# Strided Q/K loads, a re-ordered first FFN group, filler matmuls and an earlier range check in a one-core attention + FFN kernel

## The chip, the cores and the metric

The kernel runs on one core of a Trainium2 chip. The metric is the device time of one execution in microseconds (us). The core has five engines that run side by side, each through its own queue of instructions in the order of the program: TensorE (PE, matmuls and transposes, with weight loads shown as PEld), VectorE (DVE), ScalarE (ACT), GpSimd (POOL) and SyncE (SP, which here only issues DMAs). Every engine waits on semaphores for what others produce.

## The reference

Sliding-window causal attention (window 64) over 8 batches, 8 heads, 576 positions and head size 64, and behind it a multiplicative FFN with two linear layers after the product:

```python
scores = (q @ k.T) / 8                       # per batch and head
mask = (rel >= 0) & (rel < 64)               # rel = query position - key position
attn = softmax(where(mask, scores, -1e9))
x = (attn @ v) as [4608, 512]                # heads side by side
a = x @ w1                                   # 512 -> 1024
b = x @ w2                                   # 512 -> 1024
out = ((a * b) @ w3) @ w_out                 # 1024 -> 1024 -> 512, float32
```

## The kernel before

**Attention.** One batch is cut into 3 query segments of 192 positions and 4 pairs of heads, so 12 units u for each batch and 96 in all (`NU`). `scores(u)` makes two matmuls into PSUM `s_ps` (2 buffers), ACT takes the exponential of it with a fixed shift into the half-precision tile `pt` (4 buffers), and two `affine_select` groups on POOL (L271, L273) put zeros outside the window. `values(u)` makes four matmuls of V with `pt` into `o_ps` (2 buffers). V carries columns of ones, so that the sums of the exponentials come out beside the values; ACT takes their logarithm (L298, L299, into `ln_s`) and the exponential of its negative (L301, `r`), and DVE multiplies (L304, L305) into `xT`, the transposed attention output in a ring of four batches. `values` runs two units behind `scores` (`LAG = 2`). `tick(u)` is one step of both, plus the events that prepare the next batch (`late`, `second`).

**Q and K.** `load_qk` fills a float32 tile `stage` (4 buffers, shared with the weights) in four DMAs, one for each pair of heads, each to 32 partitions; a partition holds 18 positions. `cast_qk` casts half of it to half precision, `transposes` turns 6 of the 18 positions at a time: six PE transposes into one PSUM tile (`tp`, one buffer; for batch 0 `f_ps`, three buffers), then copies into `kT` (one on DVE) or `qT` (one on ACT and one on DVE, L247).

**V.** `load_v` issues five DMAs a batch from POOL, which cast on the way; `copy_v` makes block 1 from blocks 0 and 2, and half of block 4, on DVE.

**FFN.** w3 and w_out are multiplied together once (the fold, 8 steps: `fold_t` transposes 128 rows of w3, `fold_mm` multiplies with w_out), so that a group of 512 rows takes 8 steps `ffn_ab` (8 matmuls of 128x512 each, an ACT copy L379, a DVE product L380) and 4 steps `ffn_o` (8 matmuls, a DVE copy L388, a store from SP). There are 9 groups. w1, w2, w_out and w3 come as float32 megabytes through `stage` and are cast on POOL or DVE. Before the fold, w3's half-precision rows lie in the space of the first product tile and in a part of `xT` that batch 2 needs later.

**Order.** The schedule is written by hand: what is emitted first comes first in each engine's queue. Batch 0's attention runs alone in a loop (L462). Then a list of FFN steps (`slots`, 20 for group 0 with its fold, 12 for each other group) is gone through; each has a due unit, and behind each step ticks run until `u` has reached its due. In group 0 the steps before `first` have no tick behind them. The functions hung on a step by `at` run ahead of it: batch 1's casts at step 3, its k transposes at step 4, its q transposes at step 5.

**The range check.** The fixed shift of the exponential is only right if the logarithms lie in a range. `keep_sums` sends two rows of `ln_s` by DMA from SP into `lnsum` for each segment of each batch; at the end (L557 to L567) DVE squares and compares them, a small matmul adds up the flags and `bad_i` holds the count. All engines load it (L570), and a branch leads to a slow general path that these inputs do not take.

Of the kernel before, what the change touches and what calls it, by code (L numbers as in the profile page):

```python
# [15 lines left out]
P = 128  # L16
# [128 lines left out]
def kernel(  # L145
# [54 lines left out]
    def load_qk(b, which):  # L200
        src = k if which == "k" else q
        t = sb.tile([P, 2, TI * D], FP32, name="stage", bufs=4)
        for j in range(NJ):
            nc.sync.dma_start(out=t[j * TP:(j + 1) * TP],
                              in_=src[b, 2 * j:2 * j + 2].rearrange("h (p r) d -> p h (r d)", r=TI))
# [25 lines left out]
    def transposes(b, which, c, early=False):  # L231
# [7 lines left out]
        src = tp.rearrange("q i (j p) -> q j p i", p=TP)  # L239
# [37 lines left out]
    def values(u):  # L277
# [17 lines left out]
        if j == 0:  # L295
            lns[b, si] = sb.tile([P, NJ, 192], FP32, name="ln_s", bufs=3)
# [46 lines left out]
    def tick(u):  # L343
# [10 lines left out]
        if (u - LAG - 4) % 4 == 3 and u - LAG - 4 >= 8:  # L354
# [72 lines left out]
    def fold_t(fc):  # L427

        w3 = w3_rows(fc).rearrange("p a (e n) -> p (a e) n", n=P)
        tp = ps_t.tile([P, 8, P], FP16, name="tp")  # L430
# [11 lines left out]


# [7 lines left out]
    for v16 in v16s:  # L451
        nc.gpsimd.memset(v16.rearrange("p c j (a e) -> p (c j a) e", a=2)[:, :, D:2 * D], 1.0)
    wst = [load_w12(moe_w1, 0), load_w12(moe_w2, 0)]
    for which in "kq":
# [4 lines left out]
    for c in VLOADS.values():  # L459
        load_v(0, c)  # L460
    wst += [load_w12(moe_w1, 1), load_w12(moe_w2, 1)]
    for u in range(12 + LAG):  # L462
# [4 lines left out]
        if u == 5:  # L467
            pool_cp(w2_sb[:, :, 0:512], wst[1])
        if u == 6:
            dve_cp(w1_sb[:, :, 0:512], wst[0])  # L470
            load_qk(1, "k")
            load_qk(1, "q")
        if u == 10:
            pool_cp(w2_sb[:, :, 512:1024], wst[3])
            dve_cp(w1_sb[:, :, 512:1024], wst[2])
# [4 lines left out]
        if u in (9, 13):  # L480
            keep_sums((u - 9) // 4)
# [5 lines left out]
    for g in range(NG):  # L487
        part = [lambda g=g, fc=fc: ffn_ab(g, fc) for fc in range(8)]
        first = 0
        if g == 0:  # L490
            first = 5
# [15 lines left out]
            def casts_b1():  # L507
                for which in "kq":
                    for hh in range(2):
                        cast_qk(1, which, hh, pool_cp if hh else act_cp)  # L510

            def load_b1():
                for c in VLOADS.values():
                    load_v(1, c)
                for half in range(2):
                    stg["o", half] = load_wo(half)
                for n in range(4):
                    stg["3", n] = load_w3(n)
                    if n == 1:
                        for half in range(2):  # L520
                            pool_cp(wo16[:, 4 * half:4 * half + 4, :], stg["o", half])
                    if n >= 2:
                        cast_w3(n - 2, stg["3", n - 2], pool_cp)

            def more_w3(n):
                cast_w3(n, stg["3", n], pool_cp)

            part += [lambda fc=fc: fold_step(fc) for fc in range(8)]
            at(3, casts_b1)
            at(4, load_b1)  # L530
            at(4, lambda: [transposes(1, "k", c) for c in range(3)])
# [72 lines left out]
```

## Time and profile before

| | |
|---|---|
| median of three runs | 345.68 us (345.57 to 347.91) |
| the profiled execution | 346.64 us, of which the span from the first to the last instruction is 344.8 us |
| PE busy | 280.1 us, 1922 matmuls |
| DVE, ACT, POOL busy | 214.4, 211.9, 211.9 us |
| moved by DMA | 44.15 MB |

The profile is one execution. A row of the timeline gives the start, the duration, the engine, the line of the kernel, the operation with its output and input tile and shape, the count of instructions merged into the row, and in brackets how long the engine was idle before and what ended that. Merged rows can overlap the next row. A row of the stages gives the stretch, its length, the busy time of PE, PEld, DVE, ACT and POOL, the granted TensorE clock, the mean busy share of the DMA engines, and GB/s. In the list of costly groups, the numbers behind the count are busy us, mean ns of one, and idle time before. In the list of waits the columns are the total of us, the times and the longest. The strip of PE has 40 slices of 8.6 us, in tenths busy.

### The profile page before, as it was taken

What the parts mean: (1) busy time and instruction counts of PE and PEld (TensorE: products, weight loads), DVE (VectorE), ACT (ScalarE), POOL (GpSimd) and SP (SyncE); (2) the same over time, 40 slices, a digit from 0 to 9 for tenths busy, and PEclk for the clock granted to TensorE, in tenths of its full rate; (3) what the DMA queues carried; (4) which work ended last, traced back from release to release, by engine and by line L of the source; (5) the groups of instructions that cost most, each with busy time, mean ns of one, the idle gap of its engine ahead of it and who ended that gap; (6) DMA issues with size and microseconds to landing.
All of it is one profiled execution on the core that took longest, in us unless ns stands there. A gap on an engine that the chain in (4) does not pass through costs nothing.

```text
span 344.8 us, 5950 instructions
## 1 busy us (share of the span) xinstructions
PE 280.1 (81%) x1922; PEld 161.2 (47%) x1922; DVE 214.4 (62%) x393; ACT 211.9 (61%) x493; POOL 211.9 (61%) x343
## 2 busy tenths in 40 slices
PE   0425557476886799999999999999999999999950
PEld 0312323234544355555555558956555555554420
DVE  4334644526344676679789778757887876564432
ACT  1237844244553557878989887659978987843200
POOL 6375996426695465768997995659789564420000
PEclk9999999878999899999999999999999999999995
DMA  8999999997395059949977985259309202012030
GB/s 180 286 325 38 202 303 167 414 220 80 26 209 79 30 141 232 53 111 224 117 128 170 161 108 159 45 69 238 25 33 147 18 23 102 0 47 80 0 122 11
DMA packets 52201, 44.15 MB, mean 128 GB/s; under 512 B 39312, under 2 KB 39312, under 8 KB 52160
## 3 DMA queue, kind: packets, MB, share of 16 engines
q1 hardware_dynamic: 14656, 38.95, 41.6%
q0 software_dynamic: 37504, 4.72, 26.5%
q8 instruction: 17, 0.28, 0.4%
q14 instruction: 24, 0.20, 0.2%
HBM read 38.80 MB, written 9.44 MB: 140 GB/s over the span
## 4 chain that ended last, share of the span: by engine, by line
PE 68%; DVE 8%; POOL 8%; DMA 6%; ACT 4%; issue 3%; SPq 1%; DVEq 0%; ACTq 0%; POOLq 0%
PE f_ps L376 33%; PE f_ps L386 18%; PE o_ps L289 5%; PE tp L238 4%; PE s_ps L260 4%; DMA v<-in_v_dram 3%; PE f_ps L440 3%; DMA stage<-in_q_dram 3%; POOL pt L271 2%; POOL pt L273 2%; DVE kT L242 1%; DVE ab L380 1%; DVE qT L247 1%; ACT pt L264 1%; DVE xT L305 1%
## 5 line engine op out<-in xcount | busy, mean ns | idle before, releaser
L376 PE MATMUL f_ps<-xT,w_sb 128*128 128x512 f16 (+1 forms) x640 | 137.7, 366 | 1.7 <-DVE xT L305 0.6
L271 POOL TENSOR_SCALAR_AFFINE_SELECT pt<-pt 128x512 f16<-128x512 f16 (+2 forms) x128 | 65.3, 510 | 70.4 <-ACT pt L264 70.0
L376 PEld LDWEIGHTS <-w_sb 128*128 128x128 f16 x640 | 61.3, 99 | 56.1 <-issue 7.5
L264 ACT ACTIVATE pt<-s_ps 128x512 f16<-128x512 f32 (+1 forms) x96 | 53.7, 561 | 30.2 <-PE s_ps L260 25.7
L273 POOL TENSOR_SCALAR_AFFINE_SELECT pt<-pt 128x512 f16<-128x512 f16 (+2 forms) x128 | 64.4, 503 | 8.8
L386 PE MATMUL f_ps<-wc_sb,ab 128*128 128x512 f16 x288 | 68.6, 385 | 0.0
L304 DVE TENSOR_TENSOR xT<-o_ps,r 64x192 f16<-64x192 f32 x96 | 33.4, 348 | 55.5 <-ACT r L301 53.6
L380 DVE TENSOR_TENSOR ab<-f_ps,a_sb 128x512 f16<-128x512 f32 x72 | 49.7, 692 | 24.1 <-PE f_ps L376 21.4
L379 ACT COPY a_sb<-f_ps 128x512 f32<-128x512 f32 x72 | 41.3, 574 | 27.2 <-PE f_ps L376 27.2
L289 PE MATMUL o_ps<-pt,v 128*128 128x128 f16 (+1 forms) x384 | 38.0, 224 | 16.6 <-POOL pt L273 6.8
L298 ACT ACTIVATE ln_s<-o_ps 64x192 f32<-64x192 f32 x96 | 31.5, 328 | 17.5 <-PE o_ps L289 15.4
L386 PEld LDWEIGHTS <-ab 128*128 128x128 f16 x288 | 27.0, 99 | 28.2 <-issue 1.4
L260 PE MATMUL s_ps<-qT,kT 128*128 128x256 f16 x192 | 37.4, 281 | 3.1 <-DVE qT L247 2.4
L289 PEld LDWEIGHTS <-v 128*128 128x128 f16 x384 | 27.5, 101 | 22.6 <-issue 6.9
L301 ACT ACTIVATE r<-ln_s 128x192 f32<-128x192 f32 x96 | 34.9, 363 | 3.0
L305 DVE TENSOR_TENSOR xT<-o_ps,r 64x192 f16<-64x192 f32 x96 | 34.6, 361 | 1.3
L220 POOL DMA_DIRECT2D v<-in_v_dram x40 | 34.3, 862 | 1.7 <-DVE xT L305 1.1
L299 ACT ACTIVATE ln_s<-o_ps 64x192 f32<-64x192 f32 x96 | 31.0, 323 | 1.1
L260 PEld LDWEIGHTS <-kT 128*128 128x128 f16 x192 | 19.5, 104 | 22.7 <-issue 4.9
L388 DVE COPY t2k<-f_ps 128x512 f32<-128x512 f32 x36 | 24.9, 692 | 7.4 <-PE f_ps L386 6.5
L247 DVE COPY qT<-tp 64x768 f16<-64x768 f16 x21 | 20.2, 961 | 9.9 <-ACT qT L247 9.6
L242 DVE COPY kT<-tp 128x768 f16<-128x768 f16 x21 | 20.0, 951 | 4.2 <-PE tp L238 4.2
(52 smaller groups left out, 196.5 us busy)
## 6 DMA issues: line engine op xcount, KB each, us to landing
stage<-in_k_dram SPq DMA_DIRECT2D x32, 288.0 KB, 4.4
stage<-in_q_dram SPq DMA_DIRECT2D x32, 288.0 KB, 7.9
out_dram<-t2k SPq DMA_DIRECT2D x36, 256.0 KB, 2.0
stage<-in_moe_w_dram SPq DMA_DIRECT2D x8, 1024.0 KB, 10.6
v<-in_v_dram POOLq DMA_DIRECT2D x32, 128.0 KB, 4.4
stage<-in_moe_w_out_dram SPq DMA_DIRECT2D x2, 1024.0 KB
v<-in_v_dram POOLq DMA_DIRECT2D x8, 64.0 KB, 4.6
lnsum<-ln_s SPq DMA_DIRECT2D x24, 6.0 KB
```

The lines of the kernel that those rows point to most:

```text
L220: nc.gpsimd.dma_start(out=vh[lo:P, c], in_=v[b, :, s0:s0 + P - lo, :].rearrange("h s d -> s h d"))
L260: nc.tensor.matmul(s_ps[:, c0:c0 + 2 * n].rearrange("k (a n) -> k a n", a=2), kT[:, j, k0:k0 + P], qT[:, j, :, q0:q0 + n], start=True, sto ...
L264: nc.scalar.activation(pt[:, 0:2 * w], s_ps[:, 0:2 * w], AF.Exp, bias=-SHIFT, scale=scale)
L271: nc.gpsimd.affine_select(out=sl, in_=sl, pattern=[[step, nb], [0, 2], [1, n]], compare_op=ALU.is_ge, fill=0.0, base=off, channel_multipli ...
L273: nc.gpsimd.affine_select(out=sl, in_=sl, pattern=[[-step, nb], [0, 2], [-1, n]], compare_op=ALU.is_ge, fill=0.0, base=63 - off, channel_m ...
L289: nc.tensor.matmul(o_ps[:, a, q0 - q_base:q0 - q_base + n], v16[:, si * 2 + bi, j, a * D:a * D + P], pt[:, c0 + a * n:c0 + a * n + n], sta ...
L301: nc.scalar.activation(r, y[:, j], AF.Exp, scale=-1.0)
L305: nc.vector.tensor_tensor(xs[D:P], o_ps[D:P, 1, :], r[D:P], ALU.mult)
L376: nc.tensor.matmul(d[:, lo:hi], w[:, dc, fc * P:(fc + 1) * P], xT[:, dc, xc:xc + hi - lo], start=(dc == 0 and ci == 0), stop=(dc == 3), sk ...
L379: act_cp(a_sb, a_ps)
L380: nc.vector.tensor_tensor(ab[:, fc, :], b_ps, a_sb, ALU.mult)
L386: nc.tensor.matmul(o_ps, ab[:, fc, t * P:t * P + P], wc_sb[:, fc, :], start=(fc == 0), stop=(fc == 7))
```

## The change

- `load_qk` writes each pair of heads to every fourth partition (j, j+4, ...) instead of 32 adjacent ones, and the copies behind the transposes read PSUM in that order.
- Batch 0's start: the first V block is loaded between the two fills of ones; `keep_busy(n)` issues n matmuls of the identity with itself into `tp` that nobody reads: 45 ahead of the first cast, 20 behind the transposes of k and of q, 8 in each step of batch 0's loop.
- The casts of w2's first half move from POOL to DVE; the second halves of w1 and w2 are cast on DVE behind the first step of group 0. The loads of batch 1's Q and K stand one step later in the loop, and its first V block is loaded there.
- Group 0: batch 1's casts, V loads and transposes and the casts of w_out and w3 are handed out to single steps (`todo`, run behind the step), one group of transposes to a step from step 2 to step 7. w3's second half is loaded behind the casts of the first. No tick runs in the first eight steps (`first = 8`, it was 5).
- The fold's transposes use `f_ps` (three buffers) instead of `tp` (one).
- `ln_s` has four buffers; batch 0's three `keep_sums` come in group 0's steps 1 to 3.
- The last group's steps are due five units later, which finishes the ticks behind its first step; the range check is emitted behind its fifth step instead of at the end.

```diff
@@ -201,7 +201,7 @@
         src = k if which == "k" else q
         t = sb.tile([P, 2, TI * D], FP32, name="stage", bufs=4)
         for j in range(NJ):
-            nc.sync.dma_start(out=t[j * TP:(j + 1) * TP],
+            nc.sync.dma_start(out=t[j:P:NJ],
                               in_=src[b, 2 * j:2 * j + 2].rearrange("h (p r) d -> p h (r d)", r=TI))
         raws[which, b] = t
 
@@ -236,7 +236,7 @@
         tp = ps_f.tile([P, 6, P], FP16, name="f_ps") if early else ps_t.tile([P, 6, P], FP16, name="tp")
         for i in range(6):
             nc.tensor.transpose(tp[:, i, :], t16[:, 6 * c + i, :], ident16)
-        src = tp.rearrange("q i (j p) -> q j p i", p=TP)
+        src = tp.rearrange("q i (p j) -> q j p i", p=TP)
         if which == "k":
             cp = act_cp if early and c == 1 else dve_cp
             cp(kTs[b].rearrange("q j (p i) -> q j p i", i=TI)[:, :, :, 6 * c:6 * c + 6], src)
@@ -293,7 +293,7 @@
                 first = False
                 c0 += 2 * n
         if j == 0:
-            lns[b, si] = sb.tile([P, NJ, 192], FP32, name="ln_s", bufs=3)
+            lns[b, si] = sb.tile([P, NJ, 192], FP32, name="ln_s", bufs=4)
         y = lns[b, si]
         nc.scalar.activation(y[0:D, j], o_ps[D:P, 0, :], AF.Ln)
         nc.scalar.activation(y[D:P, j], o_ps[0:D, 1, :], AF.Ln)
@@ -351,7 +351,7 @@
                 event(b, *e)
         if 12 <= u - LAG < NU:
             values(u - LAG)
-        if (u - LAG - 4) % 4 == 3 and u - LAG - 4 >= 8:
+        if (u - LAG - 4) % 4 == 3 and u - LAG - 4 >= 12:
             keep_sums((u - LAG - 4) // 4)
         for e in ev:
             if e[0] != "t":
@@ -427,7 +427,7 @@
     def fold_t(fc):
 
         w3 = w3_rows(fc).rearrange("p a (e n) -> p (a e) n", n=P)
-        tp = ps_t.tile([P, 8, P], FP16, name="tp")
+        tp = ps_f.tile([P, 8, P], FP16, name="f_ps")
         for ec in range(8):
             nc.tensor.transpose(tp[:, ec, :], w3[:, ec, :], ident16)
         w3T = sb.tile([P, 8, P], FP16, name="t2k", bufs=4)
@@ -440,6 +440,27 @@
             nc.tensor.matmul(o_ps, w3T[:, ec, :], wo16[:, ec, :], start=(ec == 0), stop=(ec == 7))
         act_cp(wc_sb[:, fc, :], o_ps)
 
+    def check_sums():
+
+        rows = 2 * 3 * B
+        chk = const.tile([rows, NJ * 192], FP32)
+        nc.vector.tensor_tensor(chk, lnsum, lnsum, ALU.mult)
+        nc.vector.tensor_single_scalar(chk, chk, BOUND * BOUND, op=ALU.is_le)
+        okv = const.tile([rows, 1], FP32)
+        nc.vector.tensor_reduce(okv, chk, axis=mybir.AxisListType.X, op=ALU.min)
+        nc.vector.tensor_scalar(okv, okv, -1.0, 1.0, op0=ALU.mult, op1=ALU.add)
+        ones = const.tile([rows, 1], FP32)
+        nc.vector.memset(ones, 1.0)
+        c_ps = ps_t.tile([1, 1], FP32, name="tp")
+        nc.tensor.matmul(c_ps, okv, ones, start=True, stop=True)
+        nc.vector.tensor_copy(bad_i[0:1, :], c_ps)
+
+
+    def keep_busy(n):
+
+        d = ps_t.tile([P, P], FP32, name="tp")
+        for _ in range(n):
+            nc.tensor.matmul(d, ident16, ident16, start=True, stop=True)
 
     load_qk(0, "k")
     load_qk(0, "q")
@@ -448,15 +469,20 @@
     for qT in qTs:
         nc.vector.memset(qT[D:P, :, 0, :], 0.0)
         nc.vector.memset(qT[0:D, :, 1, :], 0.0)
-    for v16 in v16s:
+    vl = list(VLOADS.values())
+    for i, v16 in enumerate(v16s):
         nc.gpsimd.memset(v16.rearrange("p c j (a e) -> p (c j a) e", a=2)[:, :, D:2 * D], 1.0)
+        if i == 0:
+            load_v(0, vl[0])
     wst = [load_w12(moe_w1, 0), load_w12(moe_w2, 0)]
+    keep_busy(45)
     for which in "kq":
         cast_qk(0, which, 0, dve_cp)
         cast_qk(0, which, 1, act_cp if which == "k" else pool_cp)
         for c in range(3):
             transposes(0, which, c, early=True)
-    for c in VLOADS.values():
+        keep_busy(20)
+    for c in vl[1:]:
         load_v(0, c)
     wst += [load_w12(moe_w1, 1), load_w12(moe_w2, 1)]
     for u in range(12 + LAG):
@@ -465,20 +491,18 @@
         if u == 7:
             copy_v(0, 4)
         if u == 5:
-            pool_cp(w2_sb[:, :, 0:512], wst[1])
-        if u == 6:
             dve_cp(w1_sb[:, :, 0:512], wst[0])
+        if u == 7:
+            dve_cp(w2_sb[:, :, 0:512], wst[1])
             load_qk(1, "k")
             load_qk(1, "q")
-        if u == 10:
-            pool_cp(w2_sb[:, :, 512:1024], wst[3])
-            dve_cp(w1_sb[:, :, 512:1024], wst[2])
+        if u == 8:
+            load_v(1, vl[0])
         if u < 12:
             scores(u)
         if u >= LAG:
             values(u - LAG)
-        if u in (9, 13):
-            keep_sums((u - 9) // 4)
+        keep_busy(8)
     u = 12
 
 
@@ -488,7 +512,7 @@
         part = [lambda g=g, fc=fc: ffn_ab(g, fc) for fc in range(8)]
         first = 0
         if g == 0:
-            first = 5
+            first = 8
             w3Ts, stg = {}, {}
 
             def fold_step(fc):
@@ -504,67 +528,61 @@
                     f()
                 part[n] = both
 
-            def casts_b1():
-                for which in "kq":
-                    for hh in range(2):
-                        cast_qk(1, which, hh, pool_cp if hh else act_cp)
-
-            def load_b1():
-                for c in VLOADS.values():
-                    load_v(1, c)
+            def late_w12(i):
+                dve_cp((w1_sb, w2_sb)[i][:, :, 512:1024], wst[2 + i])
+
+            def first_w3():
                 for half in range(2):
                     stg["o", half] = load_wo(half)
-                for n in range(4):
+                for n in range(2):
                     stg["3", n] = load_w3(n)
-                    if n == 1:
-                        for half in range(2):
-                            pool_cp(wo16[:, 4 * half:4 * half + 4, :], stg["o", half])
-                    if n >= 2:
-                        cast_w3(n - 2, stg["3", n - 2], pool_cp)
 
             def more_w3(n):
                 cast_w3(n, stg["3", n], pool_cp)
+                if n + 2 < 4:
+                    stg["3", n + 2] = load_w3(n + 2)
+
+            def cast_wo(half):
+                pool_cp(wo16[:, 4 * half:4 * half + 4, :], stg["o", half])
 
             part += [lambda fc=fc: fold_step(fc) for fc in range(8)]
-            at(3, casts_b1)
-            at(4, load_b1)
-            at(4, lambda: [transposes(1, "k", c) for c in range(3)])
-            at(5, lambda: [transposes(1, "q", c) for c in range(3)])
-            at(5, lambda: copy_v(1, 1))
-            at(6, lambda: copy_v(1, 4))
-            at(9, lambda: more_w3(2))
-            at(11, lambda: more_w3(3))
-            at(7, lambda: load_qk(2, "k"))
-            at(8, lambda: load_qk(2, "q"))
+            todo = {
+                0: [lambda: late_w12(0), lambda: late_w12(1), lambda: cast_qk(1, "k", 0, pool_cp),
+                    lambda: cast_qk(1, "k", 1, act_cp), lambda: load_v(1, vl[1]), first_w3],
+                1: [lambda: cast_qk(1, "q", 0, pool_cp), lambda: cast_qk(1, "q", 1, act_cp),
+                    lambda: load_v(1, vl[2]), lambda: load_v(1, vl[3]), lambda: keep_sums(0)],
+                2: [lambda: transposes(1, "k", 0), lambda: load_v(1, vl[4]), lambda: keep_sums(1)],
+                3: [lambda: transposes(1, "k", 1), lambda: cast_wo(0), lambda: keep_sums(2)],
+                4: [lambda: transposes(1, "k", 2), lambda: cast_wo(1)],
+                5: [lambda: transposes(1, "q", 0), lambda: copy_v(1, 1), lambda: more_w3(0)],
+                6: [lambda: transposes(1, "q", 1), lambda: copy_v(1, 4)],
+                7: [lambda: transposes(1, "q", 2), lambda: more_w3(1), lambda: load_qk(2, "k")],
+                9: [lambda: load_qk(2, "q"), lambda: more_w3(2)],
+                11: [lambda: more_w3(3)],
+            }
         part += [lambda g=g, t=t: ffn_o(g, t) for t in range(4)]
         lo = need[g]
         hi = need[g + 1] if g + 1 < NG else NU
         for i, w in enumerate(part):
             share = max(0, i + 1 - first) / (len(part) - first)
             slots.append((w, lo + (hi - lo) * share + (LAG + 1) * (i >= first)))
-    for w, due in slots:
+    quiet = 0
+    for i, (w, due) in enumerate(slots):
         store()
         w()
+        for fn in todo.get(i, []):
+            fn()
+        if i >= len(slots) - 12:
+            due += 5
+        if u == NU + LAG + 5:
+            quiet += 1
+            if quiet == 4:
+                check_sums()
         while u < NU + LAG + 5 and u + 1 <= due + 1e-6:
             tick(u)
             u += 1
     store()
-    while u < NU + LAG + 5:
-        tick(u)
-        u += 1
-
-
-    chk = const.tile([2 * 3 * B, NJ * 192], FP32)
-    nc.vector.tensor_tensor(chk, lnsum, lnsum, ALU.mult)
-    nc.vector.tensor_single_scalar(chk, chk, BOUND * BOUND, op=ALU.is_le)
-    okv = const.tile([2 * 3 * B, 1], FP32)
-    nc.vector.tensor_reduce(okv, chk, axis=mybir.AxisListType.X, op=ALU.min)
-    nc.vector.tensor_scalar(okv, okv, -1.0, 1.0, op0=ALU.mult, op1=ALU.add)
-    ones = const.tile([2 * 3 * B, 1], FP32)
-    nc.vector.memset(ones, 1.0)
-    c_ps = ps_t.tile([1, 1], FP32, name="tp")
-    nc.tensor.matmul(c_ps, okv, ones, start=True, stop=True)
-    nc.vector.tensor_copy(bad_i[0:1, :], c_ps)
+    assert u == NU + LAG + 5 and quiet >= 4
     fast.close()
 
     bad = nc.values_load(bad_i[0:1, 0:1], min_val=0, max_val=2 * 3 * B,
```

## The prediction

> **What bounds the kernel now.** I read the page's strips first, then the busy time by stage.
>
> ```profile
> span 344.8 us, 5950 instructions
> ...
> PE   0425557476886799999999999999999999999950
> ...
> L271 POOL TENSOR_SCALAR_AFFINE_SELECT pt<-pt 128x512 f16<-128x512 f16 (+2 forms) x128 | 65.3, 510 | 70.4 <-ACT pt L264 70.0
> ...
> L273 POOL TENSOR_SCALAR_AFFINE_SELECT pt<-pt 128x512 f16<-128x512 f16 (+2 forms) x128 | 64.4, 503 | 8.8
> ...
> out_dram<-t2k SPq DMA_DIRECT2D x36, 256.0 KB, 2.0
> ```
>
> ```profile
> 8.30:13.90 5.60, 2.10 (x18) 1.84 (x18) 2.68 (x3) 1.96 (x2) 0.00 (x0) 1.00 1.02 222
> 13.90:20.00 6.10, 2.10 (x18) 1.95 (x19) 3.30 (x4) 2.21 (x3) 6.01 (x6) 1.00 1.04 386
> 36.50:46.50 10.00, 5.18 (x32) 3.18 (x32) 6.64 (x13) 7.20 (x20) 9.59 (x13) 1.00 1.03 215
> ...
> 27.57:49.58 22.01, 11.35 (x69) 6.50 (x69) 12.92 (x27) 16.53 (x45) 19.33 (x25) 1.00 0.87 164
> 49.58:80.71 31.13, 21.88 (x120) 11.05 (x119) 13.22 (x20) 12.75 (x23) 17.06 (x27) 0.89 1.35 262
> 80.71:126.87 46.16, 36.10 (x273) 21.06 (x271) 23.45 (x44) 22.72 (x53) 28.84 (x41) 0.93 0.52 84
> 126.87:332.70 205.83, 204.78 (x1423) 118.02 (x1420) 150.60 (x284) 153.13 (x365) 130.78 (x226) 1.00 0.57 101
> ```
>
> From 126.9 to 332.7 us PE is busy 204.8 of 205.8 us: that stage can only be moved, not shortened. What can be won lies ahead of it (126.9 us, where PE idles or runs slowly) and in the 12.1 us behind it. I assume that the middle keeps its 205.8 us, so a microsecond won ahead of it is won at the end. The last column is GB/s: the Q/K quarters come in at 222 and 215 GB/s, the w1/w2 halves at 386, with the DMA engines equally busy (1.02 to 1.04).
>
> **1. The start, to the first values.** The timeline of the beginning:
>
> ```profile
> 13.98 1.73 POOL L213 CAST q<-stage 128x1152 f16<-128x1152 f32 x1 [7.41 <-DMA stage<-in_q_dram]
> 15.66 4.33 POOL L220 DMA_DIRECT2D v<-in_v_dram  x5
> 15.77 2.10 PE L238 MATMUL f_ps<-ident,q 128*128 128x128 f16 x18 [4.06 <-POOL q L213]
> ...
> 20.23 0.80 PE L260 MATMUL s_ps<-qT,kT 128*128 128x256 f16 x4 [2.35 <-DVE qT L247]
> ...
> 26.07 0.29 DVE L224 COPY v<-v 64x512 f16<-64x512 f16 x1 [5.90 <-DMA v<-in_v_dram]
> ...
> 27.22 0.29 DVE L226 COPY v<-v 64x512 f16<-64x512 f16 x1 [0.86 <-DMA v<-in_v_dram]
> ...
> 28.00 0.33 ACT L298 ACTIVATE ln_s<-o_ps 64x192 f32<-64x192 f32 x1 [5.71 <-PE o_ps L289]
> ```
>
> Q lands at 13.9 us. The first values wait for V blocks 0 and 2 (26.07, 27.22), issued behind the q cast on POOL; block 0 takes 26.05 - 16.6 = 9.4 us, beside 4.2 MB of w1/w2.
> No row has a load to every fourth partition. Nearest below is the same load to adjacent partitions (222), nearest above a load to all 128 (386). I take 386, since the four strided loads together spread like that one: 2.36 MB need 6.1 us instead of 11. Counting the bytes back, they begin at 13.9 - 2.36/0.222 = 3.3 us, so q lands near 9.4. The cast on POOL (1.7) and the issue of block 2 (0.87 = 4.33/5, now first behind the cast) end at 12.0; block 0 was issued before. With 9.4 us again, block 2 lands at 21.4 at the latest; w1/w2 also end 5 us sooner, so I take 21.1: 6.1 us are gained, and the first Ln is at 21.9 instead of 28.00. Bounds: 1 us (222 GB/s, only the earlier place on POOL), and 8.7 us (V no longer last; then scores, 4 us sooner, and masks bind). The 45 and the 2 x 20 fillers (0.117 us each by the x18 row, 5.3 and 2.3 us) lie in waits: PE has nothing before k is cast, then waits for q's cast, then for the qT copies.
>
> The Trainium skill, "SBUF — State Buffer", section "Door 1: The DMA port swizzle", says that partitions 0 to 31 reach 8 of 16 ports and all 128 reach 16. Its asymptotes, 218 and 436 GB/s, agree with the rows 222 and 386. By it every fourth partition reaches 16, and at 436 the start would come 0.7 us sooner still. The Trainium skill's section "Can I just issue two DMAs to hit both halves?" lets only a transfer that spans all 128 partitions run full; its example has contiguous halves, and no run here shows a strided one.
>
> **2. Attention of batch 0** (12 values):
>
> ```profile
> 31.02 0.33 ACT L298 ACTIVATE ln_s<-o_ps 64x192 f32<-64x192 f32 x1
> ...
> 32.59 0.33 ACT L298 ACTIVATE ln_s<-o_ps 64x192 f32<-64x192 f32 x1
> ...
> 34.91 1.51 POOL L273 TENSOR_SCALAR_AFFINE_SELECT pt<-pt 128x512 f16<-128x512 f16 x1
> ...
> 37.09 0.33 ACT L298 ACTIVATE ln_s<-o_ps 64x192 f32<-64x192 f32 x1 [1.39 <-PE o_ps L289]
> ...
> 46.41 0.33 ACT L298 ACTIVATE ln_s<-o_ps 64x192 f32<-64x192 f32 x1 [1.88 <-PE o_ps L289]
> ```
>
> ACT sets the step, 32.59 - 31.02 = 1.57 us, except for two waits (1.39 and 1.88) where POOL, behind its w2 casts, was late with the masks. Those casts go to DVE, the second halves' to the FFN's first step: 1.39 + 1.88, less 0.4 for waits that stay, is -2.9. Left over: a mask that runs beside a DVE cast stretches to 1.51, and block 0 of V for batch 1 adds 0.87 on POOL; most fits into the two steps' lead of the masks, +0.4. Eight fillers a step cost 8 x 0.117 = 0.94 us of slow PE, as much PE work again as a step has (11.35/12): PE becomes the limit until its clock rises, +1.0. Sum -1.5. The step from there to the FFN is unchanged, so the FFN starts at 49.58 - 6.1 - 1.5 = 42.0 us.
>
> **3. The eight w1/w2 steps of group 0 and batch 1's transposes.**
>
> ```profile
> 49.58 8.31 PE L376 MATMUL f_ps<-xT,w_sb 128*128 128x512 f16 x29 [0.62 <-DVE xT L305]
> ```
>
> ```profile
> PE tp L238 <- DVE qT L247: 6.9, 3, 2.9
> PE tp L238 <- DVE kT L242: 5.1, 4, 1.9
> PE tp L432 <- DVE t2k L434: 4.3, 4, 2.7
> ```
>
> The second fence is who waited for whom from 49.58 to 126.87. The six transpose groups wait for their one PSUM buffer (6.9 + 5.1 us), the fold's for the same (4.3). One group to a step puts 1.73 us of matmul beside each copy.
>
> ```profile
> 84.01 0.91 PE L432 MATMUL tp<-ident,ab 128*128 128x128 f16 x8 [2.69 <-DVE t2k L434]
> ...
> 84.71 3.31 PE L440 MATMUL f_ps<-ab,t2k 128*128 128x512 f16 x8
> ...
> 91.42 2.03 POOL L425 CAST xT<-stage 128x1024 f16<-128x1024 f32 x2
> ...
> 94.32 0.61 PE L432 MATMUL tp<-ident,xT 128*128 128x128 f16 x8 [0.23 <-DVE t2k L434]
> ...
> 94.77 1.89 PE L440 MATMUL f_ps<-ab,t2k 128*128 128x512 f16 x8
> ...
> 96.49 0.38 PE L260 MATMUL s_ps<-qT,kT 128*128 128x256 f16 x2
> ...
> 96.93 0.61 PE L432 MATMUL tp<-ident,xT 128*128 128x128 f16 x8
> ...
> 105.21 2.24 POOL L213 CAST q<-stage 128x1152 f16<-128x1152 f32 x2
> ```
>
> A warm 128x512 matmul takes 0.215 us ((96.49 - 94.77)/8); the 29 of the FFN's start average 0.287: 2.1 us of slow clock, gone if the fillers keep it up. The granted clock's column (1.00 in 27.57 to 49.58) does not show this slowness, so I go by durations.
>
> The eight steps: 8 x 1.73 + 6 transpose groups x 0.34 (0.45 for eight, 94.32 to 94.77) + 1.3 for the late w1/w2 casts: they hold DVE some 3 us behind the first product, and step 3 needs the buffer that step 1's product frees. Sum 17.2: the fold starts at 59.2.
>
> **4. Fold and output of group 0, with all 15 ticks of batch 1** (before, 5 were done ahead of the fold). Work: 8 x (0.45 + 1.72) + 4 x 1.73 + 15 x 0.44 (96.49 to 96.93) + 6 x 0.34 = 32.9. Waits:
> - 0.5: the first fold's copy, nothing to run beside it.
> - 2.9: four ticks stand behind the first fold step, and two of their masks on POOL, 1.35 us a tick ((65.3 + 64.4)/96), are waited for.
> - 1.7: POOL's queue (masks, V, w3 casts of 2.03) brings w3 rows 4 to 7 late.
> - 2.6: up to batch 2's k casts POOL has 9 x 1.35 + 2 x 2.03 + 5 x 0.87 + 2 x 1.12 = 22.9 us from 63.3 on, so 86.2; PE is there at 83.6.
> - 3.9: batch 2's transposes still share one buffer.
> - 3.4: two of these waits are as long as the 2.69 us one, after which eight matmuls took 3.31 instead of 1.89 and the transposes 0.91 instead of 0.61: 1.7 each.
>
> Sum 47.9: group 1 starts at 107.1 instead of 126.87, 19.8 us sooner. Bounds: all of these waits gone, 12 us less; the 77.3 us of the old stages 3 and 4 kept whole, 12.2 us more. V, wo and w3 loads are covered by the eight steps (wo issued near 46, 4.2 MB at 386 in 10.9 us and 2 us to land: 59); SP holds behind the w3 loads only keep_sums and later loads, since no store is due. The fold's PSUM moves to the three-buffer pool (part of the 4.3). The strided PSUM read in the transpose copies keeps its innermost step; I cost it at nothing, and were a copy 0.2 us longer, the quarter of its time that DVE is idle (150.6 busy of 205.8) would cover it. The fourth ln_s buffer costs nothing and lets batch 0's three keep_sums go later on SP.
>
> **5. The range check.**
>
> ```profile
> 320.72 0.69 DVE L380 TENSOR_TENSOR ab<-f_ps,a_sb 128x512 f16<-128x512 f32 x1 [1.03 <-PE f_ps L376]
> ...
> 332.74 0.69 DVE L388 COPY t2k<-f_ps 128x512 f32<-128x512 f32 x1 [1.04 <-PE f_ps L386]
> ...
> 335.65 0.95 DVE L558 TENSOR_TENSOR chk<-lnsum 48x768 f32<-48x768 f32 x1 [2.23 <-DMA lnsum<-ln_s]
> ...
> 338.64 0.14 DVE L567 CAST bad_i<-tp 1x1 int32<-1x1 f32 x1 [0.28 <-PE tp L566]
> ```
>
> After the flag (338.78) the exit takes 6.0 us. With the flag ready early, the exit starts when the last store is issued, about 333.8 (332.74 + 0.69, and 0.4 for the issue, estimated): -5.0. Bounds: -3.3 if it waits for the store to land (2.0 us), -8 if the branch runs beside the last matmuls. But "ahead of the last group" is in it: the check stands behind step 4 of group 8, its small matmul sits in PE's queue, and step 5 is behind that. PE waits for the product (320.72 + 0.69) and the check's DVE work (338.36 - 335.65 = 2.7): 3.7 us in a stage that had no gap, plus 1.7 for the clock by the 2.69 row. +5.4 (bounds 3.0 and 5.4). Net +0.4.
>
> The Trainium skill, "TensorE: Matmul & The Clock Gate", section "What's actually happening", has the clock fall only after an idle window of about 3.4 us. This trace has it fallen after 2.69. By the Trainium skill 3.7 us of waiting would seldom hold a whole free-running window, and the net would be -1.3.
>
> **Sum** against the profiled run (346.64 us, span 344.8): -19.8 + 0.4 = -19.4, 327.2. It lies 0.96 above the median of the runs, 345.68, so 326.3.
>
> **Rivals.**
> - Strided loads stay at 222: for it, the engines were already 1.02 busy; against it, 386 at 1.04. Values start at most 1 us sooner instead of 6.1: 331.4. 0.14.
> - The fillers do not raise the clock: as in 27.57 to 49.58, where PE was half busy and stayed slow. Each step then has 0.95 + 0.94 = 1.89 us of PE instead of 1.57: 12 x 0.32 + 2.1 - 1.0 = +4.9, 331.2. Against it: 1.89 leaves no idle time. 0.10.
> - wo/w3 late: four loads now start at group 0's start, beside V's small packets; at 215 instead of 386 they land 8.7 us later, and PE, POOL's queue and the fold wait for them: 335.0. Against it, 386 came with V beside it. 0.12.
> - Slower than before: strided loads that are slower than adjacent ones. At 110 GB/s, half of 222, q lands at 24.8 instead of 9.4 (+15.4), and batch 1's q, 21.5 us behind its issue, holds ACT's casts and so the copies of group 0 by some 11 more: 352.7. It decides from about 130 GB/s down. No row speaks for it. 0.03.
> - Better: most waits of part 4 gone or the exit fully beside the matmuls: 318. 0.08.
>
> **How the numbers follow.** The forecast itself gets 0.53, from 320 to 332: the bounds of the DVE, POOL and check waits together. 320 to 336 takes in it and the first three rivals. A change of about 1% (3.5 us) is what a measurement of this kernel can tell from none. Every case but the fourth rival is over 1% faster; for waits that I have not seen I leave 0.08: 0.92 faster, 0.05 same, 0.03 slower.
>
> **What would show it.** Right: Q/K stage loads near 386 GB/s, first values near 21 us, first FFN matmuls at 0.215 us each, no wait for tp in the eight steps, group 1 near 107, a 3.7 us hole in PE within the last group, exit straight after the last store. Wrong: values still near 27 us (V or the loads), 0.4 us matmuls at the FFN's start (fillers), PE waiting for POOL's w3 cast (loads), or a middle longer than 205.8 us.

## The result, and the profile after

The changed kernel takes 336.88 us (median of four runs, 336.5 to 337.85) against 346.78 us for the kernel before on the same chip (345.57 to 347.91): a ratio of 0.9719, with a 95% interval of 0.9669 to 0.977. It is faster, as forecast, but by 10 us where 19.4 had been forecast, and the median lies 0.9 us above the upper end of the range. The profiled run took 336.5 us, its span is 334.8 us. The ratios and intervals below leave out executions more than 1.5% above the fastest of the same kernel, which happened in experiments 2, 5 and 8; the medians keep them.

The page of the changed kernel: span, PE's strip and the granted clock, 40 slices of 8.4 us.

```profile
span 334.8 us, 6342 instructions
...
PE   5727589669766999999999999999999999997890
...
PEclk9786989999979999999999999999999999999597
```

The middle is as full as before. New are the 5 in the third clock slice from the right, inside the last group, and the busier left end, part of which is filler matmuls. The timeline of the same run, at the places where the prediction put numbers:

```profile
12.64 0.76 DVE L213 CAST q<-stage 128x1152 f16<-128x1152 f32 x1 [0.43 <-DMA stage<-in_q_dram]
...
14.35 3.31 POOL L220 DMA_DIRECT2D v<-in_v_dram  x4
...
26.17 0.29 DVE L226 COPY v<-v 64x512 f16<-64x512 f16 x1 [7.30 <-DMA v<-in_v_dram]
...
26.95 0.33 ACT L298 ACTIVATE ln_s<-o_ps 64x192 f32<-64x192 f32 x1 [6.21 <-PE o_ps L289]
...
46.74 4.69 PE L376 MATMUL f_ps<-xT,w_sb 128*128 128x512 f16 x21 [0.81 <-DVE xT L305]
...
311.28 0.19 PE L455 MATMUL tp<-ones,okv 48*1 48x1 f32 x2 [3.47 <-DVE ones L453]
...
311.40 8.09 PE L376 MATMUL f_ps<-xT,w_sb 128*128 128x512 f16 x24
...
319.32 7.07 PE L386 MATMUL f_ps<-wc_sb,ab 128*128 128x512 f16 x32
...
321.97 5.51 SPq L395 DMA_DIRECT2D out_dram<-t2k  x4
```

And its stages (stretch, length, busy time of PE, PEld, DVE, ACT, POOL, granted clock, DMA share, GB/s). The borders are those of the prediction: first values, FFN's start, fold, group 1, check.

```profile
2.80:8.20 5.40, 3.61 (x34) 3.34 (x32) 2.66 (x3) 0.00 (x0) 4.80 (x3) 1.00 0.92 273
8.20:12.60 4.40, 3.19 (x33) 3.19 (x34) 2.67 (x3) 1.96 (x2) 0.00 (x0) 0.68 1.17 331
...
26.52:46.74 20.22, 14.74 (x164) 12.60 (x165) 11.84 (x27) 16.73 (x45) 16.88 (x24) 0.82 0.48 125
46.74:64.49 17.75, 15.65 (x97) 8.00 (x97) 14.23 (x17) 8.40 (x12) 8.29 (x8) 1.00 1.13 289
64.49:114.25 49.76, 36.27 (x294) 21.89 (x292) 25.84 (x49) 26.90 (x63) 36.00 (x59) 0.97 0.56 153
114.25:307.80 193.55, 192.69 (x1370) 112.63 (x1367) 145.64 (x277) 151.16 (x362) 130.36 (x226) 1.00 0.51 106
307.80:311.40 3.60, 0.13 (x3) 0.08 (x3) 3.20 (x6) 0.00 (x0) 0.00 (x0) 0.82 0.00 0
311.40:316.90 5.50, 5.50 (x15) 1.94 (x14) 0.84 (x2) 0.74 (x2) 0.00 (x0) 0.50 0.01 3
```

Read together, stage by stage against the prediction:

| Stage | predicted | measured | missing |
|---|---|---|---|
| Start: first Ln moves from 28.00 | −6.1 (to 21.9) | −1.05 (26.95) | 5.05 |
| First Ln to the FFN, 21.58 before | −1.5 | −1.8 (46.74 − 26.95 = 19.79) | −0.3 |
| The eight w1/w2 steps (with the next row 77.3 before) | 17.2 | 17.75 | 0.55 |
| Fold and output of group 0 | 47.9 | 49.76 | 1.9 |
| Check: hole and slow clock in the last group | +5.4 | +6.3 (3.5 + 2.8) | 0.9 |
| Last matmul to the end, 12.1 before | −5.0 | −3.7 (326.4 to 334.8 = 8.4) | 1.3 |
| Sum | −19.4 | −10.0 of the span | 9.4 |

The slow clock's 2.8 is what the 8.09 us for 24 matmuls have above a warm run of the same 24, 5.35 in experiment 4. The largest miss is the start: the loads and V block 2 are late, and the rest of the schedule stands where it was forecast, only later. The experiments ask why, and what the parts of the change are worth.

### The profile page after: what moved, and what is told of

It reads as the page before. It is cut to its first block, busy times and chain, and to the rows that moved or that the text cites. A ratio compares the mean times of both kernels' runs of the same rounds, so it can differ in the third digit from the quotient of the medians.

```text
span 334.8 us, 6342 instructions
## 1 busy us (share of the span) xinstructions
PE 287.5 (86%) x2119; PEld 173.3 (52%) x2119; DVE 216.5 (65%) x395; ACT 211.9 (63%) x493; POOL 207.4 (62%) x341
## 3 DMA queue, kind: packets, MB, share of 16 engines
q0 software_dynamic: 37504, 4.72, 22.8%
## 4 chain that ended last, share of the span: by engine, by line
PE 67%; DVE 9%; POOL 9%; DMA 6%; issue 3%; ACT 3%; SPq 1%; DVEq 0%; POOLq 0%; ACTq 0%
PE f_ps L376 34%; PE f_ps L386 18%; PE o_ps L289 5%; PE s_ps L260 4%; PE tp L238 4%; DMA v<-in_v_dram 4%; POOL pt L273 3%; POOL pt L271 2%; DMA stage<-in_q_dram 2%; DVE qT L247 2%; POOL v L220 1%; PE f_ps L440 1%; DVE ab L380 1%; SPq L204 1%; POOL xT L425 1%
## 5 line engine op out<-in xcount | busy, mean ns | idle before, releaser
L386 PE MATMUL f_ps<-wc_sb,ab 128*128 128x512 f16 x288 | 67.1, 379 | 0.0
L380 DVE TENSOR_TENSOR ab<-f_ps,a_sb 128x512 f16<-128x512 f32 x72 | 49.6, 691 | 21.1 <-PE f_ps L376 19.6
L289 PE MATMUL o_ps<-pt,v 128*128 128x128 f16 (+1 forms) x384 | 37.0, 219 | 12.6 <-DVE v L226 5.8
L260 PE MATMUL s_ps<-qT,kT 128*128 128x256 f16 x192 | 35.5, 268 | 2.6 <-DVE qT L247 1.9
L260 PEld LDWEIGHTS <-kT 128*128 128x128 f16 x192 | 18.5, 99 | 21.0 <-issue 3.1
```

Of the source, the lines that this page charges most:

```text
L260: nc.tensor.matmul(s_ps[:, c0:c0 + 2 * n].rearrange("k (a n) -> k a n", a=2), kT[:, j, k0:k0 + P], qT[:, j, :, q0:q0 + n], start=True, sto ...
L289: nc.tensor.matmul(o_ps[:, a, q0 - q_base:q0 - q_base + n], v16[:, si * 2 + bi, j, a * D:a * D + P], pt[:, c0 + a * n:c0 + a * n + n], sta ...
L380: nc.vector.tensor_tensor(ab[:, fc, :], b_ps, a_sb, ALU.mult)
L386: nc.tensor.matmul(o_ps, ab[:, fc, t * P:t * P + P], wc_sb[:, fc, :], start=(fc == 0), stop=(fc == 7))
```

## The experiments

Eleven kernels ran, each an edit of the changed kernel, in three jobs; the kernel before had medians of 347.16, 345.63 and 345.87 us in them (346.78 beside the changed kernel), so a difference of medians from two jobs can be off by a microsecond or so. Two profiles of the same code differ too: the changed kernel and experiments 6 and 7 are the same program up to the last group, and start group 1 at 114.25, 113.92 and 115.21 us. "Stride" stands for the Q/K loads to every fourth partition.

**1. The loads to adjacent partitions again** (first job).

```diff
-            nc.sync.dma_start(out=t[j:P:NJ],
+            nc.sync.dma_start(out=t[j * TP:(j + 1) * TP],
...
-        src = tp.rearrange("q i (p j) -> q j p i", p=TP)
+        src = tp.rearrange("q i (j p) -> q j p i", p=TP)
```

> The changed kernel with Q/K loaded to adjacent partitions again. In the changed kernel q landed at 12.6 us (13.9 before) and V block 2 at 26.2. Theory A (shared engines: V block 2 lands when the 4.2 MB of w1/w2 that share each DMA engine with it are drained, so the loads count only through the end of that traffic): q near 15, V block 2 near 28, total +1.5 to +3 us (338.5 to 340). Theory B (the strided loads reach the w1/w2 rate and are worth what the prediction said, hidden by something else): q near 15 and total +5 (342). Theory C (stride is worth nothing): total within 1 us of 336.9.

343.85 us, ratio 0.9882 (0.9835 to 0.993): the stride alone is worth 6 to 7 us (7.0 by the medians, 5.7 by the ratios), more than its gain at the start. The timeline of this run:

```profile
14.24 0.76 DVE L213 CAST q<-stage 128x1152 f16<-128x1152 f32 x1 [1.38 <-DMA stage<-in_q_dram]
...
29.52 0.29 DVE L226 COPY v<-v 64x512 f16<-64x512 f16 x1 [8.74 <-DMA v<-in_v_dram]
...
52.08 1.85 POOL L213 CAST q<-stage 128x1152 f16<-128x1152 f32 x1 [2.92 <-DMA stage<-in_q_dram]
53.88 3.18 POOL L220 DMA_DIRECT2D v<-in_v_dram  x3
...
70.22 0.55 DVE L224 COPY v<-v 64x512 f16<-64x512 f16 x1 [3.26 <-DMA v<-in_v_dram]
...
73.27 3.34 PE L440 MATMUL f_ps<-ab,t2k 128*128 128x512 f16 x8 [4.84 <-DVE t2k L434]
...
122.55 3.62 PE L376 MATMUL f_ps<-xT,w_sb 128*128 128x512 f16 x16
```

The start loses 29.52 − 26.17 = 3.35 us. By group 1 it is 122.55 − 114.25 = 8.3. The other five are lost in one chain: batch 1's q lands late, POOL waits 2.92 us for it ahead of its cast, batch 1's V blocks are issued behind that cast (at 53.88, and now behind the loads of w_out that SP issues from 52.96 on; in the changed kernel at 46.90, ahead of them at 50.41), DVE waits 3.26 us for one of them, and the copy of the first fold's transposes stands behind that copy in DVE's queue. PE waits 4.84 us (1.73 in the changed kernel) and then runs eight matmuls in 3.34 instead of 1.9 us, together 4.5 of the five.

**2. Is q held up by the weights?** SP's queue waits for q before it issues w1 and w2 (third job).

```diff
+    seen = const.tile([NJ, D], FP32)
+    nc.sync.dma_start(out=seen, in_=raws["q", 0][0:NJ, 0, 0:D])
     wst = [load_w12(moe_w1, 0), load_w12(moe_w2, 0)]
```

> The changed kernel, except that SP's queue waits for batch 0's q (a copy of a few of its numbers on the same queue) before it issues the first halves of w1 and w2, so that beside the Q/K loads only V block 0 is in flight. In the changed kernel q landed at 12.64 us, not at 9.4, although the engines moved 378 GB/s over 10 to 12.6: more than 0.5 MB of what they moved by then was not q and k. Theory A (the w loads, issued from 6.16 us, share the DMA engines with q and hold it back): q lands at 10.5 to 11.3 and its cast starts there; V block 2, with less of w ahead of it or beside it in the same order, lands 0 to 1.5 us earlier than 26.17. Theory B (a load that touches every fourth partition is slow by itself, whatever lies beside it): q lands within 0.5 us of 12.64, with the rate over its last stretch well under 300 GB/s, and w1 and w2 are simply 6 us later, so that the FFN waits for them: 338 to 341. By A 333 to 338, for w lands later but is first needed at scores step 5.

SP's rows, and then the stages:

```profile
3.58 2.70 SPq L204 DMA_DIRECT2D stage<-in_q_dram  x4
12.32 0.78 SPq L478 DMA_DIRECT2D seen<-stage  x1
13.14 2.27 SPq L402 DMA_DIRECT2D stage<-in_moe_w_dram  x4
```

```profile
2.80:8.20 5.40, 2.69 (x34) 2.51 (x32) 2.67 (x4) 0.03 (x1) 4.80 (x3) 0.96 0.89 268
8.20:12.40 4.20, 3.02 (x29) 3.02 (x30) 2.59 (x4) 1.94 (x2) 0.00 (x1) 0.50 0.88 228
```

With the weights out of the way q still lands at 12.3, and its cast starts at 12.3 to 12.6 in the three profiles of like code, so they were not what held it: with only V block 0 beside it the strided load moves 268, then 228 GB/s, (5.4 × 268 + 4.2 × 228) KB over 9.6 us = 250 on average, where the adjacent one had 222 and the load to 128 partitions 386. The second theory holds for the load, though not its consequence: the weights came in time for the FFN (46.85 against 46.74). Group 1 starts 1.7 us later (115.97), little more than the 1.3 between profiles of like code. 336.89 us, ratio 0.9723 (0.966 to 0.9787). V block 2 landed at 26.61, no sooner for having less of w1/w2 ahead of it.

**3. V block 0 back behind q's cast** (second job).

```diff
-        if i == 0:
-            load_v(0, vl[0])
...
-    for c in vl[1:]:
+    for c in vl:
         load_v(0, c)
```

> The changed kernel with V block 0 issued behind q's cast again, with the other four. Theory A (block 0's small packets, early, slow the Q load beside them: q landed at 12.6 us in the changed kernel, and at 13.3 with two early blocks): q near 12.0 or sooner, block 2 near 27, total 336.5 to 338.5 us. Rival (the strided load alone reaches the w1/w2 rate once nothing runs beside it, as the prediction took it): q near 9.4 and block 2 near 23, total 333 to 335.

```profile
11.77 1.14 POOL L213 CAST q<-stage 128x1152 f16<-128x1152 f32 x1 [5.20 <-DMA stage<-in_q_dram]
...
26.54 0.29 DVE L226 COPY v<-v 64x512 f16<-64x512 f16 x1 [0.41 <-DMA v<-in_v_dram]
```

In the timeline of this run q is 0.9 us earlier and V block 2 0.4 us later (it is copied at 25.37 to 26.17 in the three profiles of like code): the early V block 0 shared the engines with q and won nothing, since block 2 is the one that is waited for. 334.99 us, ratio 0.9688 (0.9609 to 0.9768), 1.9 us under the changed kernel by the medians and 1.1 by the ratios, with intervals that overlap; at group 1 it is 1.5 us ahead (112.77).

**4. V block 2 first.** Its load goes out right behind block 0's, at 4.9 us, instead of behind q's cast (first job).

```diff
             load_v(0, vl[0])
+            load_v(0, vl[1])
...
-    for c in vl[1:]:
+    for c in vl[2:]:
```

> V block 2 is issued right behind block 0, ahead of the second fill of ones, so near 5 us instead of 14.4. Theory A (drain of the w1/w2 traffic at about 23.5 us sets the landing): it still lands after 20, first values at 20 to 24, total 331 to 335, and q lands 1 us later. Theory B (9 to 12 us from issue): it lands near 17, the first values wait for scores and masks at about 22, total 332 to 333. Theory C (own packets, four blocks together): as B, since only two blocks are ahead.

```profile
14.97 2.43 POOL L220 DMA_DIRECT2D v<-in_v_dram  x3
...
19.52 0.29 DVE L226 COPY v<-v 64x512 f16<-64x512 f16 x1
...
41.82 4.69 PE L376 MATMUL f_ps<-xT,w_sb 128*128 128x512 f16 x21 [0.81 <-DVE xT L305]
...
307.82 0.18 PE L455 MATMUL tp<-ones,okv 48*1 48x1 f32 x2 [3.46 <-DVE ones L453]
307.94 5.35 PE L376 MATMUL f_ps<-xT,w_sb 128*128 128x512 f16 x24
```

The copy of V block 2 shows no wait any more in the timeline, at 19.52, and the FFN starts at 41.82: that is the 42.0 of the prediction, reached by another way. 330.74 us, ratio 0.9546 (0.9509 to 0.9583): 6.1 us better than the changed kernel. Of the 4.9 us at the FFN's start the fold stage gives 1.3 back (group 1 at 110.70, 3.6 us earlier). The 24 matmuls behind the hole took 5.35 us in this run: the clock did not fall, and these 2.7 us of its span have nothing to do with V.

**5. The second halves of w1 and w2 wait for V block 2** (first job): SP copies a few numbers of it before it issues them.

```diff
         load_v(0, c)
+    seen = const.tile([P, D], FP16)
+    nc.sync.dma_start(out=seen[0:1, :], in_=v16s[0][0:1, 2, 0, 0:D])
     wst += [load_w12(moe_w1, 1), load_w12(moe_w2, 1)]
```

> The second halves of w1 and w2 (2.1 MB) wait on SP until V block 2 has landed. Theory A (V block 2's packets wait behind w1/w2 packets on every engine): it lands near 19 to 21 instead of 26.2 us, and the total is 330 to 332. Theory B (9 to 12 us from issue to landing whatever runs beside): it lands at 24 to 26, total 335 to 337. Theory C (the four V blocks' own small packets set it): lands near 21 to 23, total 332 to 334.

```profile
14.71 3.31 POOL L220 DMA_DIRECT2D v<-in_v_dram  x4
...
20.50 0.41 DVE L226 COPY v<-v 64x512 f16<-64x512 f16 x1 [0.95 <-DMA v<-in_v_dram]
...
41.98 4.69 PE L376 MATMUL f_ps<-xT,w_sb 128*128 128x512 f16 x21 [0.81 <-DVE xT L305]
```

Issued at 14.71, later than in the changed kernel, V block 2 lands after 5.8 us instead of 26.17 − 14.35 = 11.8. What it waits for is the w1/w2 traffic that shares the engines with it. 332.92 us, ratio 0.9535 (0.9493 to 0.9578); the late weights give 2.1 us back in the fold stage (111.78 − 59.87 = 51.9).

**6. The check's small matmul behind the last store**, its DVE work left where it is (first job).

```diff
-        c_ps = ps_t.tile([1, 1], FP32, name="tp")
-        nc.tensor.matmul(c_ps, okv, ones, start=True, stop=True)
-        nc.vector.tensor_copy(bad_i[0:1, :], c_ps)
+        return okv, ones
...
     store()
+    count_sums(*flags)
```

(`count_sums` holds the three lines taken out.)

> The check's DVE work stays behind step 5 of the last group, its matmul and the flag's copy go behind the last store. Theory A (the hole of 3.5 us and the 5.5 us at half clock behind it cost 6.3 us, all because the small matmul stands ahead of the FFN's in PE's queue): no hole in the last group, and 330.5 to 331.5 us. Rival (the DVE work itself delays the products of the last steps, or the exit waits for a flag that now comes last): 333 to 336 us.

The timeline of PE:

```profile
298.81 13.98 PE L376 MATMUL f_ps<-xT,w_sb 128*128 128x512 f16 x64
312.62 7.07 PE L386 MATMUL f_ps<-wc_sb,ab 128*128 128x512 f16 x32
319.62 0.19 PE L458 MATMUL tp<-ones,okv 48*1 48x1 f32 x2
```

All 64 matmuls run in 13.98 us without a gap, and the time is 330.56 us, ratio 0.9551 (0.9503 to 0.9598), 6.3 us better. The last stretch, from the end of PE's 32 matmuls (319.7) to the span's end (327.1), is 7.4 us; in the changed kernel, with the flag ready at 311.7, it is 8.4. So the span's 334.8 − 327.1 = 7.7 us are 6.3 of hole and clock, 1.0 of exit and 0.3 by which group 1 was earlier (113.92).

**7. The whole check at the end again** (second job): `check_sums()` behind the last `store()`.

```diff
-            if quiet == 4:
-                check_sums()
...
     store()
+    check_sums()
```

> The changed kernel with the whole range check behind the last store again (its last sums are still sent early). Theory A (moved ahead, the check costs 3.5 us of hole and 2.8 us of slow clock, and gives back 3.7 us at the exit): no hole, PE done 6.3 us sooner, an exit longer by the check's 2.7 us of DVE work and its small steps, total 333 to 335. Rival (the move is worth what the exit shows, 3.7 us): 339 to 341.

The timeline of PE:

```profile
299.98 13.98 PE L376 MATMUL f_ps<-xT,w_sb 128*128 128x512 f16 x64
...
324.25 0.18 PE L455 MATMUL tp<-ones,okv 48*1 48x1 f32 x2 [3.40 <-DVE ones L453]
```

332.73 us, ratio 0.9619 (0.9538 to 0.97): 4.2 us faster than the changed kernel by the medians and 3.5 by the ratios, and 2.2 slower than experiment 6, though those two intervals overlap. Hole and slow clock are gone here too (6.3 us), and from PE's last FFN matmul to the end it is 9.9 us instead of 8.4. So this part of the change cost 3 to 5 us as it was made, and its DVE half alone, with PE's part late, looks like a gain of 2.

**8. No filler matmuls** (second job, `range(n)` to `range(0)` in `keep_busy`; third job, the same edit with experiments 4 and 6 in, beside a partner with fillers).

> The changed kernel with no filler matmuls. Theory A (they keep TensorE's clock up to the FFN and cost almost nothing in the loop): the first FFN matmuls take 0.43 us instead of 0.22 for some 3.5 us, the loop keeps its step, total +1 to +2.5 us (338 to 339.5). Rival (PE's extra work in the loop costs as much as the clock gives): the loop is shorter by 1 to 2 us, total within 1 us of 336.9.

> The same kernel as its partner in this job (V block 2 first, the check's matmul last), without any filler matmul. Theory A (the fillers keep the clock up through the waits ahead of the first values, as the prediction had it): the 21 matmuls at the head of the FFN's first step take 6 to 8 us instead of about 4.7, the loop's last steps lengthen by 0 to 1 us, and the time is 1.5 to 4.5 us over the partner's. Theory B (what the fillers save at the head of the FFN they cost in the loop, where they stand in PE's queue ahead of the scores): within 0.7 us of the partner.

On the changed kernel it gave 336.77 us with runs from 330.28 to 338.95, ratio 0.9606 (0.9485 to 0.9727), too wide to tell. Beside its partner, six runs each: 326.05 us without (ratio 0.9411, 0.9374 to 0.9448) and 326.1 with (0.9408, 0.9363 to 0.9452). The fillers do warm the head of the FFN, 5.22 us without and 4.69 with (6.61 without them in the profile of the first pair, a run of 338.95 us). From V block 2's copy to the FFN's start it is 22.9 us without (20.48 to 43.34) and 22.3 with (20.13 to 42.38). The two profiles end 1.0 us apart (spans of 325.0 and 324.0), the medians 0.05: in the whole time the fillers are worth nothing that could be measured. The timeline row without them, and below it that of the partner:

```profile
43.34 5.22 PE L376 MATMUL f_ps<-xT,w_sb 128*128 128x512 f16 x21 [0.62 <-DVE xT L305]
...
42.38 4.69 PE L376 MATMUL f_ps<-xT,w_sb 128*128 128x512 f16 x21 [0.81 <-DVE xT L305]
```

**9. Experiments 4 and 6 together** (second job; again in the third as the partner above).

> V block 2 issued early and the check's small matmul last, together. Theory A (the two lie in different stages and add up: -4 to -6 for V, -6.3 for the matmul): 325 to 328 us. Rival (what V wins at the start is lost again to a later wait in the fold): 329 to 331.

> The changed kernel with V block 2's load issued right behind block 0's and with the range check's matmul and the copy of its flag behind the last store, once more, as the partner of the run without filler matmuls. It should come to 326 to 327, as it did (326.3).

326.3 us (325.81 to 326.52), ratio 0.9421 (0.9349 to 0.9493), and 326.1 (323.02 to 327.06) the second time. That is 10.6 us better than the changed kernel, about the 3.6 us that experiment 4 had won by group 1 and the 6.3 of experiment 6, and 4.3 better than experiment 6 alone. The 3.6 is from one pair of profiles: group 1 starts at 110.70 to 111.79 in the three with V block 2 early and the fillers in, and at 113.92 to 115.21 in the three of the changed kernel's code. This kernel beats both that the change is between.

## Why the prediction came out as it did

**Where it failed: step 1, the start.** "I take 386, since the four strided loads together spread like that one." They do not: with only V block 0 beside them they averaged 250 GB/s (experiment 2), a gain of 13% over the adjacent 222, not 74%. With only the weights beside them q's cast began at 11.77 (experiment 3); by the prediction's own count of 2.36 MB from 3.3 us on that is about 280 GB/s, an estimate. No run had them quite alone. So q's cast began at 12.64 instead of 9.4, 3.2 us late; about 0.9 of it is V block 0, which shares the engines with q (experiment 3). Adjacent loads (experiment 1) put it at 14.24. The second half of the step was V block 2's 9.4 us from issue to landing: it took 11.0 from the end of its issue (14.35 + 0.83 to 26.17), beside w1/w2, where the forecast's 21.1 left it 9.1. The forecast had counted on w1/w2 ending sooner; experiment 5 shows that it is these that hold V back: counted from the start of its issue, block 2 took 5.8 us with half of them out of the way and 11.8 with all of them. Together 5.05 us. The start came out as that of the rival "strided loads stay at 222" (1 us gained), though the loads were faster than that.

The Trainium skill, "SBUF — State Buffer", section "Door 1: The DMA port swizzle", by which every fourth partition would reach all 16 ports and 436 GB/s, does not agree with these rows (268, 228). Its section "Can I just issue two DMAs to hit both halves?", which keeps the full rate to a single transfer over all 128 partitions, is nearer, but a load of 32 partitions spread out was still faster than one of 32 side by side. The row of 386 that the prediction counted as agreeing with 436 lies 50 GB/s below it.

**Step 2, the loop**: right, −1.8 against −1.5. The fillers were costed at +1.0 there and −2.1 at the FFN's head. The second was seen, with a size of 0.5 (experiment 8; 1.9 in the profile of its first kernel); the first was not, and their sum is zero within a microsecond.

**Step 3, the eight steps**: right, 17.75 against 17.2, and no slow matmul at their head (4.69/21 = 0.223 us).

**Step 4, the fold stage**: 49.76 against 47.9. The kinds of waits were the forecast ones, and three were longer. The list of waits of the changed kernel, 64.49 to 114.25 (total us, times, longest):

```profile
PE tp L238 <- POOL k L213: 3.5, 1, 3.5
PE tp L238 <- DVE qT L247: 3.0, 1, 3.0
PE tp L238 <- DVE kT L242: 2.1, 2, 1.1
PE f_ps L440 <- DVE t2k L434: 2.1, 2, 1.7
```

Batch 2's k casts were waited for 3.5 us, not 2.6; its transposes 5.1 (3.0 + 2.1), not 3.9; the copies of the fold's transposes 2.1, not 0.5. The w3 rows cost 0.3, not 1.7. (POOL's work ahead of the k casts adds up to 22.8 us in the prediction's terms, not 22.9.) Not in the prediction's sum at all is how much of this stage hung on the stride: five of the 8.3 us that experiment 1 had lost by group 1 lie here, through batch 1's q and its V blocks. I had priced the stride only at the start; only the rival with slower loads counted batch 1's q.

**Step 5, the check**: the hole was right (3.47 us against 3.7), its slow clock was mis-sized: 2.8 us instead of 1.7, since the clock stayed at 0.50 for 5.5 us of the matmuls behind the hole and I had taken the eight matmuls of one row as its whole length. The exit was mis-sized too, −3.7 instead of −5.0, near the bound (−3.3) for an exit that waits for the last store: 7.3 us pass from that store's issue (321.97 + 5.51) to the end, where the forecast had the 6.0 that followed the flag before. The trace shows that wait. From the list of waits of SP's queue in the changed kernel, and from the rows of the branch (L590):

```profile
SPq L590 <- SPq L590: 1.7, 1, 1.7
...
L590 SPq EVENT_SEMAPHORE  x8: 17/17/17, 328.2 to 330.4; - x8
```

Among these eight is the semaphore of the last store, and SP gets past it 3.07 us after it began to issue that store; in experiment 6 the same wait is 0.6 us and ends 2.02 us after. So the exit does wait for the store, for 3.07 us where the bound had 2.0, and 4.5 us follow instead of 6.0. Net +2.6 instead of +0.4: 2.2 us. That the part is a loss in sum is shown by experiments 6 and 7. The hole is 3.46 to 3.47 us long in every run that has it. Behind it the 24 matmuls took 7.94 to 8.15 us in the changed kernel, in experiments 1, 3 and 5 and in the first kernel of experiment 8, and 5.35 in experiments 2 and 4, where the clock did not fall. Where it fell, it did so 2.0 to 2.5 us after the last matmul ahead of the hole (in the changed kernel at 310.1, with PE idle from 307.8), and it stayed at 0.50 for 6.8 us. The Trainium skill, "TensorE: Matmul & The Clock Gate", section "What's actually happening", would let the clock fall after a whole idle window of about 3.4 us; the trace does not agree.

**The range** took in the rivals one at a time. A start that fails by 5 us together with small misses of one sign in four other rows of the table was not in it.

## What to carry to other kernels

A load that is issued sooner or runs faster is worth what it frees behind it: follow its data through every queue (here POOL's issue of V, then DVE's copies, then the fold) before putting a price on it, in later batches too. Of several transfers that are needed together, move first the one that is waited for last: sending V block 2 ahead won about 3.6 us by group 1 with one moved line, where sending block 0 ahead had won nothing. Work that needs PE for 0.2 us behind 3 us of another engine belongs where PE has nothing queued behind it; only its other engines' part should go early.

## What the runs showed that I had not expected

- A strided load of 32 partitions also takes longer to issue: the four of q took 2.70 us of SP's queue (experiment 2), against 1.84 for the same four to adjacent partitions (experiment 1) and 2.27 for the four full weight loads of 1 MB each (experiment 2).
- A 128 KB V load lands 5.8 us after its issue with 2 MB of weights issued ahead of it (experiment 5), and after 11.8 (the changed kernel) or 12.5 (experiment 2, issued at 14.09) with 4 MB.
- With the flag ready long before the end, the stretch from PE's last matmul to the end is 8.3 to 8.6 us (the changed kernel and experiments 1 to 5); with the flag's matmul behind the last store it is 7.2 to 7.4 (experiments 6 and 9). The microsecond lies in SP's wait for the last store at the branch, which ends 3.1 to 3.3 us after the store's issue with an early flag and 2.0 after it with a late one. Why the store takes longer to be seen as landed there stays open.
- Why a load to every fourth partition stays near 250 GB/s, whether by its packets or by the engines that they fall to, stays open.
